# One load of all of w_in, half of batch 0 first, and a deeper ring between the two products

## The chip, the cores and the metric

The kernel runs on one core of a Trainium2 chip. TensorE (PE) multiplies matrices, VectorE (DVE), ScalarE (ACT) and GpSimd (POOL) do elementwise work, SyncE (SP) issues the transfers between the chip's memory and the core's (SBUF); products land in PSUM. The metric is the device time of one execution in microseconds (us). Before the change the median of three runs is 1023.45 us (1021.89 to 1024.68).

## The reference

The inputs are queries, keys and values of 8 batches, 8 heads, 512 local and 32 global tokens of 64 elements, and the weights of an MLP, w_in (512 x 2048) and w_out (2048 x 512), as float64. Local tokens attend to the 32 global ones and to the local ones at a distance of at most 32; global tokens attend to all.

```python
s_ll = np.where(abs(pos[:, None] - pos[None, :]) <= 32, scale * q_l @ k_l.T, -1e9)
a_l = sm(concat([scale * q_l @ k_g.T, s_ll]))        # sm: softmax with 1e-9 in the divisor
out_l = a_l @ concat([v_g, v_l])
out_g = sm(scale * q_g @ concat([k_g, k_l]).T) @ concat([v_g, v_l])
x = concat([out_g, out_l])                           # (8 * 544) tokens x 512
h = x @ w_in
y = (h * np.cos(h)) @ w_out
```

## The kernel before

Heads go in pairs, so a batch has 4 pairs, whose two heads fill 128 partitions. Tokens of a batch go in 4 query tiles of 128; a tile's keys are a window of 192 or 224 columns, so a query tile has two blocks of keys to transpose. Batches 0 and 1 (FB) have attention in float32: f_qk (L605ff) makes the scores, f_tt adds the mask and takes the negative minimum on DVE (L629), f_ex exponentiates and sums on ACT (L438), f_nm multiplies by the reciprocal of the sum on POOL (L655), f_tr transposes on PE (L670) and copies the result out of PSUM (L678), f_av multiplies with v (L698), and f_av_b splits the result into two float16 tiles, xh and xl, with the scale xsf (L715, L716). The functions fg_* do the same for global tokens. Batches 2 to 7 use float16 pairs of high and low words (sc_*, av_a) and transposing transfers.

The MLP runs over 17 chunks, 16 of 256 local tokens and one of all 256 global tokens, each in 8 steps. A step's first product, m1, is 24 matmuls (L1094: xh by wi_h, xl by wi_h, xh by wi_l) into the tile ph; then ACT (u, L1116), DVE (u, L1117), ACT (Sin, L438), POOL (square, L1129), DVE (gf, L1131), ACT (gh, L1135) and POOL (gl, L1136) make h * cos(h) in two words; the second product, m2, is 12 matmuls (L1150 to L1152). It stands `lag` = 3 steps behind m1, through a ring of 4 tiles gh and gl.

The weights are decoded from raw float64. For each piece DVE takes the maximum of its high words (raw_max, L288), then low words (L263, L266), ACT or DVE combine them (L237, L268), ACT casts the high float16 word (L281) and POOL subtracts for the low one (L231). w_in has 8 pieces of 128 x 1024, w_out 16 of 128 x 512. Raw pieces lie in places that are free until later: in the tiles of w_out (wo_h, wo_l) and in a ring of two. The pieces 6 and 7 of w_in are loaded when earlier ones have been decoded. w_in_done (L358ff) reduces the maxima of all pieces across the partitions (a matmul with ones, pm_wi) and makes from them the scale of x (xs, and f_xs's xsf, L603) by a chain of small DVE operations. Before it, no xh exists and no m1 can run.

The order of the work is written as events: `at(slot, phase, f, ...)` puts a function into a slot, one slot to a step of m1, negative ones ahead of the first. The functions are emitted by slot and phase, and a scheduler then orders each engine's instructions with this as their priority.

## Time and profile before

| | |
|---|---|
| median of three runs | 1023.45 us |
| profiled execution | 1027.77 us, span 1026.0 us |
| busy, share of the span | PE 90%, DVE 63%, ACT 63%, POOL 60% |
| granted TensorE clock, mean | 0.949 of 2.4 GHz |
| first matmul of m1 | 94.07 us |

Times in the rows below are those of the profiled execution, from its span's start. A row of the time line or of a table by lines gives busy time; idle time before an instruction stands in brackets or behind the bar, with what ended it. PE's busy time includes time at a low clock: at half the clock the same matmuls are busy twice as long, so work is compared by counts of matmuls and not by busy time alone.

### The profile page before, as it was taken

What the parts mean: (1) busy time and instruction counts of PE and PEld (TensorE: products, weight loads), DVE (VectorE), ACT (ScalarE), POOL (GpSimd) and SP (SyncE); (2) the same over time, 40 slices, a digit from 0 to 9 for tenths busy, and PEclk for the clock granted to TensorE, in tenths of its full rate; (3) what the DMA queues carried; (4) which work ended last, traced back from release to release, by engine and by line L of the source; (5) the groups of instructions that cost most, each with busy time, mean ns of one, the idle gap of its engine ahead of it and who ended that gap; (6) DMA issues with size and microseconds to landing.
All of it is one profiled execution on the core that took longest, in us unless ns stands there. A gap on an engine that the chain in (4) does not pass through costs nothing.

```text
span 1026.0 us, 20740 instructions
## 1 busy us (share of the span) xinstructions
PE 928.3 (90%) x7847; PEld 631.5 (62%) x7847; DVE 645.5 (63%) x1575; ACT 644.9 (63%) x1298; POOL 617.8 (60%) x817
## 2 busy tenths in 40 slices
PE   7864788899898889998999999998999999999996
PEld 5543456566566566766676666665666666666663
DVE  5975867467757767857585767666867644422231
ACT  6543787556667676865777577766685866444341
POOL 4472564645675956674767577767676778344442
PEclk9656898999999999999999999999999999999999
DMA  9348013044546464455545553555454423000000
GB/s 374 123 169 329 18 42 108 1 122 115 115 91 148 74 169 91 106 105 141 124 91 124 142 123 91 124 142 124 90 110 102 101 45 75 2 22 21 1 22 20
DMA packets 141147, 106.11 MB, mean 103 GB/s; under 512 B 120440, under 2 KB 120440, under 8 KB 139000
## 3 DMA queue, kind: packets, MB, share of 16 engines
q1 hardware_dynamic: 141048, 104.80, 39.8%
q8 instruction: 61, 1.00, 0.4%
q14 instruction: 38, 0.31, 0.1%
HBM read 51.82 MB, written 8.91 MB: 59 GB/s over the span
## 4 chain that ended last, share of the span: by engine, by line
PE 32%; DVE 18%; POOL 16%; DMA 13%; ACT 12%; issue 7%; SPq 1%; POOLq 0%; ACTq 0%; DVEq 0%
PE ph L1094 13%; POOL planes L881 6%; POOL t L871 6%; PE po L1152 5%; PE po L1150 5%; PE po L1151 5%; DMA qkr<-qk 5%; ACT t L438 4%; DMA vr<-v 4%; DVE kl L535 3%; POOL w L1129 2%; ACT L438 2%; DMA wo_h<-wo 2%; DVE u L1117 2%; DVE qm L494 2%
## 5 line engine op out<-in xcount | busy, mean ns | idle before, releaser
L1094 PE MATMUL ph<-xh,wi_h 128*128 128x256 f16 x1024 | 282.1, 276 | 15.9 <-DVE gf L1131 10.3
L1094 PE MATMUL ph<-xl,wi_h 128*128 128x256 f16 x1024 | 281.8, 275 | 0.9 <-DVE xl L716 0.9
L1094 PE MATMUL ph<-xh,wi_l 128*128 128x256 f16 x1024 | 281.8, 275 | 0.0
L1136 POOL TENSOR_TENSOR gl<-gf,gh 128x512 f16<-128x512 f32 x136 | 160.2, 1181 | 145.2 <-ACT gh L1135 142.5
L1094 PEld LDWEIGHTS <-wi_h 128*128 128x128 f16 x2176 | 211.5, 99 | 57.0 <-issue 23.0
L1150 PE MATMUL po<-wo_h,gh 128*128 128x512 f16 x544 | 208.6, 383 | 12.2 <-ACT o L1160 9.8
L1151 PE MATMUL po<-wo_l,gh 128*128 128x512 f16 x544 | 208.5, 383 | 0.0
L1152 PE MATMUL po<-wo_h,gl 128*128 128x512 f16 x544 | 203.1, 382 | 1.1 <-POOL gl L1136 1.0
L1129 POOL TENSOR_TENSOR w<-w 128x512 f32<-128x512 f32 x136 | 144.6, 1064 | 87.8 <-ACT w L438 84.9
L1117 DVE SCALAR_TENSOR_TENSOR u<-u,cm,ph 128x512 f32<-128x512 f32 x136 | 101.2, 744 | 132.9 <-ACT u L1116 132.7
L1131 DVE SCALAR_TENSOR_TENSOR gf<-w,ph 128x512 f32<-128x512 f32 x136 | 93.1, 685 | 108.6 <-POOL w L1129 108.0
L1135 ACT CAST gh<-gf 128x512 f16<-128x512 f32 x136 | 82.5, 613 | 120.6 <-DVE gf L1131 119.1
L438 ACT ACTIVATE t<-t,mn 128x224 f32<-128x224 f32 (+1 forms) x256 | 117.2, 459 | 50.8 <-DVE mn L809 39.8
L438 ACT ACTIVATE w<-u,ca 128x512 f32<-128x512 f32 x136 | 97.9, 721 | 81.1 <-DVE u L1117 77.0
L871 POOL TENSOR_TENSOR t<-t,sm 128x192 f32<-128x192 f32 (+1 forms) x192 | 101.0, 559 | 73.3 <-DVE sm L856 73.3
L881 POOL TENSOR_TENSOR planes<-t,planes 128x192 f16<-128x192 f32 (+1 forms) x192 | 118.3, 646 | 0.0
L1094 PEld LDWEIGHTS <-wi_l 128*128 128x128 f16 x1088 | 107.4, 99 | 16.7 <-issue 2.0
L1116 ACT ACTIVATE u<-ph,cm 128x512 f32<-128x512 f32 x136 | 92.5, 680 | 20.5 <-PE ph L1094 19.6
L1152 PEld LDWEIGHTS <-gl 128*128 128x128 f16 x544 | 53.6, 98 | 65.5 <-POOL gl L1136 2.5
L1151 PEld LDWEIGHTS <-gh 128*128 128x128 f16 x544 | 53.7, 99 | 64.0 <-issue 15.3
L1150 PEld LDWEIGHTS <-gh 128*128 128x128 f16 x544 | 53.7, 99 | 48.4 <-issue 2.7
L809 DVE CUSTOM_DVE_ANT_0 t<-ps,msk,al 128x192 f32<-128x192 f32 (+1 forms) x192 | 75.6, 427 | 5.9 <-PE ps L793 5.8
(203 smaller groups left out, 1433.6 us busy)
## 6 DMA issues: line engine op xcount, KB each, us to landing
qkr<-qk SPq DMA_DIRECT2D x24, 608.0 KB, 4.8
vr<-v SPq DMA_DIRECT2D x8, 1280.0 KB, 7.3
out<-o SPq DMA_DIRECT2D x34, 256.0 KB, 2.2
kh<-qa SPq DMA_DIRECT2D x48, 152.0 KB, 2.7
...
```

The source lines that it names most:

```text
L438: ins = nc.scalar.activation(*a, **k).ins
L871: nc.gpsimd.tensor_tensor(t[:, h], t[:, h], rb[:, h], op=ALU.mult)
L881: nc.gpsimd.tensor_tensor(lo[:, h], t[:, h], hi[:, h], op=ALU.subtract)
L1094: nc.tensor.matmul(ph[:, a], w[:, kc, f], x[:, kc, q], start=first and ip == 0, stop=last and ip == 2, skip_group_check=True,)
L1116: nc.scalar.activation(u, ph, AF.Identity, bias=m)
L1117: nc.vector.scalar_tensor_tensor(u, u, m, ph, op0=ALU.subtract, op1=ALU.subtract)
L1129: nc.gpsimd.tensor_tensor(w, w, w, op=ALU.mult)
L1131: nc.vector.scalar_tensor_tensor(gf, w, 0.5, st.pop(("ph", c, j)).rearrange("p a b -> p (a b)"), op0=ALU.subtract, op1=ALU.mult,)
L1136: nc.gpsimd.tensor_tensor(gl, gf, gh, op=ALU.subtract)
L1150: nc.tensor.matmul(po[k], gh[:, q], wo_h[:, f], start=(f == 0), stop=False)
L1151: nc.tensor.matmul(po[k], gh[:, q], wo_l[:, f], start=False, stop=False)
L1152: nc.tensor.matmul(po[k], gl[:, q], wo_h[:, f], start=False, stop=(f == NJ - 1))
```

## The change

- All 8 pieces of w_in are loaded at the start, without a wait between them: pieces 1 and 3 lie in the static tiles of the planes and of v, piece 7 in xh and xl of the second set, the others in wo_h, wo_l and one raw tile. Ahead of and between them only half the columns (352 of 608) of batch 0's queries and keys are loaded (load_half), and the mask as 16-bit words, without a copy by ACT. The second halves follow w_in.
- Batch 0's first two query tiles of all four pairs are done ahead of w_in_done; the other two, and the global tokens, stand between the first steps of m1. f_x now makes xh and xl for half a batch.
- A fence on DVE: what is emitted behind w_in_done and f_xs, up to slot 10, is ordered behind them on that engine. Only the even pieces of w_in are decoded ahead of it, the odd ones in slots 0 to 3.
- f_nm no longer multiplies the 4 tiles of scores (192 or 224 columns); it multiplies the identity by the reciprocals into 4 diagonal tiles of 128 x 128, and f_tr's transposes become float32 matmuls with these. All windows are 224 wide.
- m2 stands 11 steps behind m1 in chunks 0 and 1 and 6 afterwards; the ring of gh and gl has 11 tiles; 5 slots without m1 lie between chunks 1 and 2. w_out's maxima, scale and decode move to slots 4 to 17, batch 1 to slots 10 and on.
- Code that was switched off is gone, and a scratch area of transfers is smaller, which frees SBUF.

```diff
-WOORD = (12, 13, 14, 15, 8, 9, 10, 11, 4, 5, 6, 7, 0, 1, 2, 3)
+FTE = ((1, 1, 0, 0), (0, 0, 0, 0))
+ZH = 352
+WOORD = (8, 10, 12, 14, 9, 11, 13, 15, 0, 2, 4, 6, 1, 3, 5, 7)
+SH = 5
+LAGR = 11
+LAG = 6
+NG = 11
 MASK = -(2.0**120)
...
+            if k == 7:
+                for i, tag in enumerate(("xh", "xl")):
+                    t = ap_.tile([P, NPAIR, SL], F16, tag=tag, name=f"raw_wi7{tag}")
+                    raw = wfs["raw", k, i] = t.rearrange("p a b -> p (a b)").bitcast(I64)
+                    nc.sync.dma_start(raw, wi[kc * P : (kc + 1) * P, 1024 + 512 * i : 1536 + 512 * i])
+                return
+            if k == 1:
+                raw = plx.rearrange("p a b c d -> p (a b c d)").bitcast(I64)
+            elif k == 3:
+                raw = vhlf[:, :4096].bitcast(I64)
+            elif k == 5:
+                raw = w1.tile([P, 1024], I64, tag="raw1", name="raw_wi5", bufs=1)
+            else:
+                t, half = {0: (wo_h, 0), 2: (wo_h, 1), 4: (wo_l, 0), 6: (wo_l, 1)}[k]
                 raw = t[:, 8 * half : 8 * half + 8].rearrange("p a b -> p (a b)").bitcast(I64)
-            loads[k] = nc.sync.dma_start(raw, wi[kc * P : (kc + 1) * P, c])
+            nc.sync.dma_start(raw, wi[kc * P : (kc + 1) * P, c])
             wfs["raw", k] = raw
-
-        maxes, loads = {}, {}
 
         def w_in_max(k):
             kc = k // 2
-            if k % 2 == 0:
-                wfs["s", kc] = w1.tile([P, 3], F32, tag="ws3", name=f"ws3_{kc}", bufs=4)
...
+            sm = st.pop(("fsm", b, p, hf))
             nc.vector.tensor_scalar(sm, sm, 1e-9, None, op0=ALU.add)
             nc.vector.reciprocal(sm, sm)
-            for i in range(2):
-                for h in range(2):
-                    c = 2 * i + h
-                    nc.gpsimd.tensor_scalar(
-                        ts[i][:, h], ts[i][:, h], sm[:, c : c + 1], 1.0, op0=ALU.mult, op1=ALU.mult
-                    )
+            dg = ap_.tile(
+                [P, 4, P], F32, tag=("gt", "ptg")[(p + hf) % 2], name=f"dg_{b}_{p}_{hf}", bufs=1
+            )
+            for c in range(4):
+                nc.gpsimd.tensor_scalar(
+                    dg[:, c], ident, sm[:, c : c + 1], 1.0, op0=ALU.mult, op1=ALU.mult
+                )
+            st["dg", b, p, hf] = dg
...
-                    w = WINF[2 * hf + i][1] - P if k else P
                     for h in range(2):
-                        nc.tensor.transpose(
-                            tr[:w, 2 * i + h], ts[i][:, h, k * P : k * P + w], ident
+                        nc.tensor.matmul(
+                            tr[:w, 2 * i + h], ts[i][:, h, k * P : k * P + w], dg[:, 2 * i + h],
+                            start=(i + h == 0), stop=(i + h == 2), skip_group_check=True,
                         )
-                if k and hf == 0:
...
         def m1_d(c, j):
             w = st.pop(("u", c, j))[1]
             n = w.shape[-1]
-            gh = mp.tile([P, n], F16, tag="gh", name=f"gh_{c}_{j}", bufs=4)
-            gl = mp.tile([P, n], F16, tag="gl", name=f"gl_{c}_{j}", bufs=4)
+            s = (NS * c + j) % NG
+            pool = mp if s < 4 else mp2
+            gh = pool.tile([P, n], F16, tag="gh", name=f"gh_{c}_{j}", bufs=4 if s < 4 else NG - 4)
...
+        def fence():
+            fences.append(last("DVE"))
...
+        H = -40
+        for f, *a in (
+            (load_qk, 0, 0), (load_mask,), (load_qk, 0, 1), (w_in_load, 0), (load_qk, 0, 2),
+            (w_in_load, 1), (load_qk, 0, 3), (w_in_load, 2), (w_in_load, 3), (load_v, 0), (w_in_load, 4), (w_in_load, 5),
+            (w_in_load, 6), (w_in_load, 7),
+        ):
+            at(H, PA, f, *a)
+        for p in range(NPAIR):
+            at(H, PB, load_half, 0, p, ZH, NZ)
+        for p in range(NPAIR):
+            f_qt(H + 1 + p, 0, p, 0)
+            at(H + 2 + p, PA2, f_tr, 0, p, 0)
+            at(H + 3 + p, PA2, f_av, 0, p, 0)
+        for k in range(8):
+            at(H + 10, PA, w_in_max, k)
+            if k % 2:
+                at(H + 10, PA, w_in_piece, k - 1)
+            if k == 3:
+                at(H + 10, PA, v_a, 0)
+                at(H + 10, PA, v_b, 0)
+                at(H + 10, PA, v_c, 0)
+        at(H + 11, PA, w_in_done)
+        at(H + 11, PD, f_xs, 0)
+        at(H + 11, PE_, fence)
+        for p in range(NPAIR):
+            at(H + 12, PF, f_x, 0, p, 0)
+        for n, k in enumerate((1, 3, 5, 7)):
+            at(n, PG, w_in_piece, k)
+        at(3, PJ, zero_planes)
+        for p in range(NPAIR):
+            u = (1, 2, 4, 5)[p]
+            e = 3 + 3 * (p // 2)
+            f_qt(u, 0, p, 1, e - u)
+            at(e + 1, PA2, f_tr, 0, p, 1)
+            at(e + 1, PC, f_av, 0, p, 1)
+            at(e + 1, PF, f_x, 0, p, 1)
+        for g in range(2):
...
                 at(s, mb, m1_b, c, j)
-                at(s + 1, mc, m1_c, c, j)
-                at(s + 1, md, m1_d, c, j)
-                at(s + lag, m2, m2_a, c, j)
+                s1 = s + 1 if c > 1 else NS * c + j // 2 * 2 + 2 if c else (3, 3, 3, 6, 6, 6, 8, 8)[j]
+                at(s1, mc, m1_c, c, j)
+                at(s1, md, m1_d, c, j)
+                at(m + j, m2, m2_a, c, j)
+            at(m + NS - 1, ob, chunk_out_scale, c)
             for k in range(CT // P):
-                at(NS * c + NS - 1 + lag, ob, m2_b, c, k)
...
             if s == CE:
                 end = len(nc.cur_bb.bb.instructions)
             for _, _, f, a in sorted(ev[s], key=lambda e: e[:2]):
+                n = len(nc.cur_bb.bb.instructions)
                 f(*a)
+                if fences and s < 10:
+                    for ins in list(nc.cur_bb.bb.instructions)[n:]:
+                        if ins.engine == mybir.EngineType.DVE:
+                            tc.add_manual_dep(ins, fences[-1].name, order, reason="fence")
```

SP's queue of transfers at the start of the program, of the kernel before (wi is w_in, qkf the queries and keys of batches 0 and 1, raw_wi a raw piece; wo_h and wo_l take raw pieces of w_in here):

```order
L328 DMA wo_h<-wi 128x1024 x2
L461 DMA vr_125<-v 128x2560
L448 DMA qf_2_127<-qkf 128x608
L449 DMA kf_2_128<-qkf 128x608
L328 DMA wo_l<-wi 128x1024
L448 DMA qf_3_133<-qkf 128x608
L328 DMA wo_l<-wi 128x1024
L449 DMA kf_3_134<-qkf 128x608
L328 DMA raw_wi_137<-wi 128x1024
L328 DMA raw_wi_139<-wi 128x1024
L328 DMA wo_h<-wi 128x1024
L328 DMA wo_l<-wi 128x1024
```

and of the kernel after:

```order
L346 DMA wo_h<-wi 128x1024
L490 DMA qf_2_123<-qkf 128x352
L490 DMA kf_2_124<-qkf 128x352
L346 DMA plx<-wi 128x1024
L490 DMA qf_3_128<-qkf 128x352
L490 DMA kf_3_129<-qkf 128x352
L346 DMA wo_h<-wi 128x1024
L346 DMA vhl<-wi 128x1024
L494 DMA vr_134<-v 128x2560
L346 DMA wo_l<-wi 128x1024
L346 DMA raw_wi_137<-wi 128x1024
L346 DMA wo_l<-wi 128x1024
```

In the first excerpt whole queries and keys (608 columns) stand between the pieces, and the last two stand behind two others whose place or decode they need; in the second all pieces stand in a row with half queries and keys (352), and v ahead of the last ones.

TensorE around the scale of x and the first matmul of m1 (pm_wi: the maximum across partitions; ph_0: the first step), of the kernel before:

```order
L760 MATMUL fgtr_1_0_632<-ident,planes_g 128x128 x4
L760 MATMUL fgtr_1_1_638<-ident,planes_g 128x128
L775 MATMUL gacc_1_641<-fptg_1_631,vr_125 64x32 x8
L194 LDWEIGHTS ones
L194 MATMUL pm_wi<-d_wi,ones 128x128
L194 LDWEIGHTS ones
L194 MATMUL pm_wj<-d_wj,ones 128x128
L775 MATMUL gacc_1_641<-fptg_1_631,vr_125 64x32 x12
L1094 LDWEIGHTS wi_h
L1094 MATMUL ph_0_900<-xh_836,wi_h 128x256
```

and of the kernel after:

```order
L728 MATMUL acc_0_1_305<-ptb,vr_134 64x128 x4
L728 MATMUL acc_0_1_305<-ptb,vr_134 64x64 x2
L728 MATMUL acc_0_1_305<-ptb,vr_134 64x128 x2
L394 LDWEIGHTS ones
L394 MATMUL pm_wi<-d_wi,ones 128x256
L647 MATMUL fps_0_1_0_535<-qkr_0_114 128x224
L647 MATMUL fps_0_1_1_536<-qkr_0_114 128x224
L647 MATMUL fps_0_1_0_535<-qkr_0_114 128x224
L647 MATMUL fps_0_1_1_536<-qkr_0_114 128x224
L647 MATMUL fps_1_1_0_588<-kf_1_119,qf_1_118 128x224 x2
L1067 LDWEIGHTS wi_h
L1067 MATMUL ph_0_466<-xh_450,wi_h 128x256
```

Before, all of batch 0 and its global tokens (fgps, fgtr, gacc) stand ahead of pm_wi; after, pm_wi follows the first half's products with v (acc_0_1), and the second half's scores (fps_0_1) are mixed with the first matmuls of ph_0.

VectorE around the scale xsf (wos: a maximum of w_out; lo_wi: low words of a piece of w_in; L716 and later L746: xl), of the kernel before:

```order
L288 TENSOR_REDUCE wos<-wo_h 128x1
L1075 TENSOR_SCALAR ca_892<-hsc,pvs 128x1
L389 TENSOR_SCALAR xs<-xs,gam 128x4
L390 TENSOR_SCALAR xs_95<-xs_95,gam 128x4
L208 TENSOR_SCALAR cm_893<-ca_892 128x1
L603 TENSOR_SCALAR xsf<-xs,pvr_735 128x4
L1077 TENSOR_SCALAR cm_893<-cm_893 128x1
L1078 TENSOR_SCALAR ca_892<-ca_892 128x1
L716 SCALAR_TENSOR_TENSOR xl_837<-acc_0_314,xsf,xh_836 128x512
L716 SCALAR_TENSOR_TENSOR xl_837<-acc_1_405,xsf,xh_836 128x512
L288 TENSOR_REDUCE wos<-wo_h 128x1
L716 SCALAR_TENSOR_TENSOR xl_837<-acc_2_521,xsf,xh_836 128x512
```

and of the kernel after:

```order
L418 TENSOR_SCALAR xs<-xs,gam 128x4
L632 TENSOR_SCALAR xsf<-xs,pvr_447 128x4
L1042 TENSOR_SCALAR ca_460<-hsc,pvs 128x1
L267 TENSOR_SCALAR lo_wi_496<-plx 128x1024
L270 TENSOR_SCALAR lo_wi_496<-plx 128x1024
L661 ISA t_0_2_542,mn_0_1_541<-fps_0_1_0_535,msk,alf 128x224
L661 ISA mn_0_1_541 128x1
L661 ISA t_0_2_542,mn_0_1_541<-fps_0_1_1_536,msk,alf 128x224
```

Before, the chain is mixed with maxima of w_out and the xl of all four pairs follow; after, the chain stands alone, and the decode of an odd piece and the mask of the second half's scores come behind it, ahead of the first xl.

## Rows read from the trace of the kernel before

**Rows 1.** The page's first parts: busy time of each engine over the span, and the GB/s that the DMA engines moved in 40 slices of 25.65 us.

```profile
PE 928.3 (90%) x7847; PEld 631.5 (62%) x7847; DVE 645.5 (63%) x1575; ACT 644.9 (63%) x1298; POOL 617.8 (60%) x817
...
GB/s 374 123 169 329 18 42 108 1 122 115 115 91 148 74 169 91 106 105 141 124 91 124 142 123 91 124 142 124 90 110 102 101 45 75 2 22 21 1 22 20
```

**Rows 2.** The table by stretches of the whole trace. Columns: stretch in us, its length, busy us and number of instructions of PE, PE's weight loads, DVE, ACT and POOL, the granted TensorE clock, DMA share, GB/s.

```profile
0.00:40.00 40.00, 29.82 (x144) 21.39 (x144) 28.39 (x105) 21.90 (x65) 17.97 (x43) 0.93 0.73 290
40.00:100.00 60.00, 36.01 (x262) 23.75 (x263) 45.39 (x118) 28.48 (x53) 29.84 (x40) 0.53 0.63 230
100.00:120.00 20.00, 12.41 (x82) 9.21 (x79) 16.35 (x59) 13.55 (x32) 7.94 (x12) 0.83 0.09 28
120.00:240.00 120.00, 108.42 (x839) 74.39 (x839) 80.42 (x191) 82.55 (x158) 64.41 (x85) 0.93 0.24 77
240.00:400.00 160.00, 143.87 (x1291) 97.90 (x1289) 112.40 (x271) 109.07 (x229) 107.67 (x145) 0.98 0.52 114
400.00:960.00 560.00, 541.80 (x4874) 369.26 (x4872) 347.17 (x814) 368.45 (x733) 368.01 (x475) 0.99 0.41 92
960.00:1016.00 56.00, 55.96 (x367) 35.62 (x364) 14.63 (x21) 20.85 (x31) 21.98 (x20) 1.00 0.03 10
1016.00:1026.00 10.00, 0.00 (x0) 0.00 (x0) 0.75 (x1) 0.00 (x0) 0.00 (x0) 0.76 0.17 52
```

**Rows 3.** The same table for the instructions of line L1094 alone (the first product): busy us of its matmuls (x records) and of its weight loads, the granted clock, DMA share, GB/s.

```profile
0.00:120.00 120.00, 10.48 (x72) 7.90 (x72) 0.72 0.57 216
120.00:240.00 120.00, 40.25 (x315) 31.55 (x316) 0.93 0.24 77
```

**Rows 4.** The same for line L1150, a third of the second product.

```profile
120.00:240.00 120.00, 20.23 (x52) 5.18 (x52) 0.93 0.24 77
```

**Rows 5.** The chain that ended last, near its end: start us, us, what. The first product's 24 matmuls of two neighbouring steps.

```profile
997.77 2.62 PE ph L1094 x24
...
1002.98 2.62 PE ph L1094 x24
```

**Rows 6.** The time line of PE: start us, us from the first start to the last end, engine, line, operation, out<-in, shapes, number of records, and in brackets the idle time before with its releaser.

```profile
94.07 0.37 PE L1094 MATMUL ph<-xh,wi_h 128*128 128x256 f16 x1 [5.57 <-ACT xh L715]
...
106.37 2.88 PE L614 MATMUL fps<-qkr 64*128 64x192 f32 x16
...
129.00 2.06 PE L698 MATMUL acc<-fpt,vr 128*64 128x128 f32 x32
...
138.13 0.60 PE L670 MATMUL ftr<-ident,t 128*128 128x128 f32 x4
```

**Rows 7.** The time line of SP's queue and of DVE: the issues of the last two pieces of w_in and the maximum of the last.

```profile
23.54 0.33 SPq L328 DMA_DIRECT2D wo_h<-wi  x1
39.78 0.33 SPq L328 DMA_DIRECT2D wo_l<-wi  x1
...
47.35 1.21 DVE L288 TENSOR_REDUCE ws<-wo_l 128x1 f32<-128x1024 f32 x1
```

**Rows 8.** The time line around the scale of x (DVE, and the ACT instruction that it releases).

```profile
87.00 0.29 DVE L196 TENSOR_REDUCE r_wi<-pm_wi 128x1 f32<-128x128 f32 x1 [2.46 <-PE pm_wi L194]
...
87.40 0.14 DVE L311 TENSOR_SCALAR wr_i<-r_wi 128x1 f32<-128x1 f32 x1
87.58 0.15 DVE L312 TENSOR_SCALAR wr_i<-wr_i 128x1 uint32<-128x1 uint32 x1
...
93.07 0.22 DVE L603 TENSOR_SCALAR xsf<-xs,pvr 128x4 f32<-128x4 f32 x1
...
93.33 1.84 ACT L715 ACTIVATE xh<-acc,xsf 128x512 f16<-128x512 f32 x3 [7.29 <-DVE xsf L603]
```

**Rows 9.** The page's costliest groups, the instructions of one MLP step on DVE and ACT: line, engine, operation, out<-in, shapes, count | busy us, mean ns of one | idle us before, releaser.

```profile
L1117 DVE SCALAR_TENSOR_TENSOR u<-u,cm,ph 128x512 f32<-128x512 f32 x136 | 101.2, 744 | 132.9 <-ACT u L1116 132.7
L1131 DVE SCALAR_TENSOR_TENSOR gf<-w,ph 128x512 f32<-128x512 f32 x136 | 93.1, 685 | 108.6 <-POOL w L1129 108.0
L1135 ACT CAST gh<-gf 128x512 f16<-128x512 f32 x136 | 82.5, 613 | 120.6 <-DVE gf L1131 119.1
...
L438 ACT ACTIVATE w<-u,ca 128x512 f32<-128x512 f32 x136 | 97.9, 721 | 81.1 <-DVE u L1117 77.0
...
L1116 ACT ACTIVATE u<-ph,cm 128x512 f32<-128x512 f32 x136 | 92.5, 680 | 20.5 <-PE ph L1094 19.6
```

**Rows 10.** The time line of DVE and POOL at two decodes of w_in.

```profile
35.36 0.90 DVE L263 TENSOR_SCALAR lo_wi<-raw_wi 128x1024 uint16<-128x1024 uint16 x1
...
59.20 3.33 DVE L263 TENSOR_SCALAR lo_wi<-raw_wi 128x1024 uint16<-128x1024 uint16 x1
...
59.38 2.56 POOL L231 TENSOR_TENSOR wi_l<-y_wi,wi_h 128x256 f16<-128x256 f32 x4
```

**Rows 11.** The table by stretches for 40 to 100 us in three slices, columns as in rows 2.

```profile
40.00:60.00 20.00, 16.37 (x95) 9.85 (x96) 16.51 (x46) 12.93 (x28) 13.03 (x19) 0.50 0.50 169
60.00:80.00 20.00, 10.24 (x97) 7.18 (x95) 17.64 (x34) 8.92 (x10) 13.55 (x17) 0.59 0.42 141
80.00:100.00 20.00, 9.40 (x72) 6.72 (x73) 11.23 (x40) 6.63 (x16) 3.25 (x5) 0.51 0.96 380
```

**Rows 12.** Groups of instructions by line and shape on DVE in the first 240 us, columns as in rows 9.

```profile
L629 DVE CUSTOM_DVE_ANT_0 t<-fps,msk,alf 128x224 f32<-128x224 f32 x48 | 19.9, 446 | 0.2
...
L288 DVE TENSOR_REDUCE wos<-wo_h 128x1 f32<-128x512 f32 x8 | 5.5, 682 | 6.3 <-DMA wo_h<-wo 6.1
```

More of the change, by code (lines that the diff above doesn't have):

```diff
@@ L607, in f_qk @@
             pt = [
[L608 removed]
+                ps.tile(
+                    [P, 2, FW], F32, tag="ph" if (b, hf, h) == (0, 0, 1) else "att",
+                    name=f"fps_{b}_{p}_{hf}_{h}",
+                )
+                for h in range(2)
             ]
@@ new lines, in f_g, with load_mask, zero_planes, slot0 @@
+        def f_g(u, b, g):
+            at(u, PG, fg_a, b, g)
+            at(u, PG, fg_b, b, g)
+            at(u + 1, PG, fg_c, b, g)
+            at(u + 1, PG, fg_d, b, g)
+        def load_mask():
+            nc.sync.dma_start(msk.bitcast(U16), mask)
+        def fence():
+            fences.append(last("DVE"))
+        def zero_planes():
+            for i in range(4):
+                nc.gpsimd.memset(planes[i], 0.0)
+        def slot0(c):
+            return NS * c + (SH if c > 1 else 0)
@@ new lines, in body, with last @@
+        fences = []
+        def last(e):
+            return [i for i in nc.cur_bb.bb.instructions if i.engine == getattr(mybir.EngineType, e)][-1]
+        H = -40
[7 more added lines that the diff above has]
+            at(H, PB, load_half, 0, p, ZH, NZ)
```

450 lines of the change are left out of this document (180 added, 270 removed).

## The prediction

> **What bounds the kernel now.** I read the table by stretches first [rows 2]. From 960 us on TensorE is never idle, and 400 to 960 us has it busy 97%; the last 10 us have no matmul at all. So the end of the run is set by how much TensorE work is left at 400 us, and time can be won only where TensorE waits or runs slowly, which is before 400 us. The granted clock tells the second half of the story: 0.93 in the first 40 us, 0.53 from 40 to 100 us, 0.98 and more after 240 us. A clock of 0.53 is nearer to the level of 1.2 GHz than to 2.4 GHz. Over the span the engines are busy 90% (PE) and 60 to 63% (the three others) [rows 1].
>
> Next I counted work instead of busy time. One step of the MLP is 24 matmuls of the first product (2.62 us at full clock) and 12 of the second, a period of 5.21 us, so the second half takes 2.59 us [rows 5]. Until 240 us the trace has 72 + 315 = 387 matmuls of L1094 [rows 3], 390 with those that the trace misses, or 16.25 steps, and 52 of L1150 [rows 4], 4 in a step, which with a few lost records makes 13.5 steps. At full clock that is 16.25 x 2.62 + 13.5 x 2.59 = 77.5 us. The attention of batches 0 and 1 by unit rows [rows 6]: a score matmul is two records of 2.88/16 = 0.18 us, a transpose one of 0.15, an attention-times-v product two of 2.06/32 = 0.064. The code issues 64, 128 and 128 of them for two batches: 23 + 19 + 16 = 58 us, and about 14 for the global tokens, 72 together or 36 per batch. With 2 us of batch 2 the work done by 240 us is worth 151.5 us. TensorE thus lost 88 us before 240 us, where the change acts.
>
> The reason stands in two views. w_in's last two pieces are issued at 23.54 and 39.78 us, the last maximum runs at 47.35 [rows 7], the cross-partition maximum is read at 87.00, the scale of x is there at 93.07 [rows 8], and the first MLP matmul starts at 94.07 [rows 6]. Until then the MLP has no work, and the second product waits longer, since its weights are decoded after.
>
> **The change part by part.**
>
> *Loads (stage A).* SP now issues 1.44 MB of half queries and keys, 0.23 MB of mask, 8.39 MB of w_in and 1.31 MB of v with no wait between: 11.4 MB. At the 374 GB/s of the first slice [rows 1] that is 30.4 us; with 3 to 4 us to start and land, 34 us. By the 290 GB/s of the first 40 us [rows 2] it is 39 us plus the same: these are my bounds, 34 and 43, and I take 34 because the queue is no longer interrupted. VectorE has to do by then 8 maxima at 1.21 [rows 7], four even pieces at 3 us, 16 score reductions at 0.446 [rows 12] and small ones, about 31 us in all, so it may be late by a few. Behind the last maximum stands a chain of some 18 dependent small operations at the 0.18 us of [rows 8] (87.40, 87.58), a hop through PE, and the rest of one decode: 7 us. The scale is ready at about 41 us, against 93.07. The fence only keeps other DVE work behind this chain; what it holds back (second half scores, odd pieces) has no one waiting before 41 us. The mask copy dropped from ACT is counted at nothing, since ACT's work there lies beside the loads.
>
> *From 41 us to the first m2 (stage B).* In PE's order twelve steps of m1, the second half of batch 0 and its global tokens come before the first second product. TensorE's work in it is 12 x 2.62 + 18 + 4 = 53 us. VectorE's is larger: 12 steps of 0.744 + 0.685 us = 17.1 [rows 9]; four odd pieces with three 1024-wide operations between 0.90 [rows 10] and 1.21 us [rows 7], 12; 16 maxima of w_out at 0.68, 10.9; 16 score reductions at 0.446, 7.1 [rows 12]; some 24 small ones (copies, xl, sums, scales), 10: 57 us. ScalarE's is about the same: 12 steps of 0.680 + 0.721 + 0.613 = 24.2 [rows 9], and 30 for exponentials, table loads and casts. VectorE was busy 76% in 40 to 100 us and 67% in 120 to 240 [rows 2], with the same kind of work in both; I take 75%, so 76 us, and the first m2 starts near 117 us instead of 127. From 0.82 (100 to 120 us) to 0.67 the range is 70 to 85 us. The 8.39 MB of w_out queue behind w_in and the second halves (1.05 MB): by the same 374 GB/s they are in by about 63 us, before their scale is wanted at step 9, so I cost them at nothing; if they were late, the first m2 would be, not m1.
>
> *To the state that the kernel before has at 240 us (stage C).* What is left is 4.25 steps of m1 (11), 13.5 of m2 (35), batch 1 (36) and batch 2's 2 us: 84 us. The normalising matmul adds to it. It is a full float32 product where a transpose was: a score product of 192 columns takes 2 x 0.18 us, so 128 columns about 0.24, against 0.15 [rows 6]: +0.09 on 64 in each batch, 6 us here. The bounds are nothing (if a plain matmul costs what a transpose does) and +0.21 each, 13 us (if it costs a whole score product). The Trainium skill (TensorE: Matmul & The Clock Gate, section "Terms") calls the transpose mode four times faster for float32. By it a product would take 0.60 us and stage C 29 us more, but the score rows give a ratio of 1.6, so I don't follow it. POOL scales 128 columns instead of 192 or 224, which is cheaper by a little. So 90 us of work. In 120 to 240 us the kernel before did 315/24 = 13.1 steps of m1, 13 of m2 and about 32 us of attention, 100 us of work in 120, a share of 0.84 [rows 2 to 4]. 90/0.84 = 107 us: the state is reached at 224 us, 16 to 17 us sooner. With 0.80 and 0.90 it is 112 and 100 us.
>
> *After it.* The deeper ring of g and the lag of 6 or 11 steps let m2 wait less, while attention beyond it stands in PE's order as before; 240 to 400 us lost about 15 us, 400 to 960 about 23 us [rows 2]. What of the first bit is regained I count at nothing, since ACT and POOL each have as much work per step there as PE; if the ring does cover it, it is worth up to 10. The last 66 us keep.
>
> Sum: profiled run 1027.8 - 17 = 1011 us. It lies 4.3 us above the median of the runs shown, so 1006 us.
>
> **The rivals.**
>
> *The ring and the early start pay in full.* Stage B at 0.82 ends at 111 us; with m2 eleven steps behind, PE always finds ready work and stage C runs at 0.97 as 400 to 960 us did [rows 2]: 93 us, state at 204, 36 us sooner, and the ring wins back two thirds of the 15 us lost in 240 to 400. 1023.5 - 46 = 977. For it: the weights' decodes no longer stand between m1 and m2. Against: VectorE and ScalarE are still the fuller ones.
>
> *The gain is given back.* Batch 2's attention has the same chain of ACT, POOL and transposing DMAs; if it sets the time after 240 us, PE arrives early and waits there. The end stays, near 1023. For it: the lost 15 us in 240 to 400 with the other engines at 67 to 70% [rows 2].
>
> *Slower: TensorE stays at the low clock in stage B.* From 40 to 100 us the granted clock was 0.50, 0.59 and 0.51, with PE busy only half to four fifths of these slices [rows 11]. Stage B now has PE waiting on VectorE for small pieces again. If all its 53 us of work run at 1.2 GHz they take 106, the stage ends at 147 and the state is reached 14 us later than before: 1023.5 + 14 = 1037. It decides from a share x of low clock where 53(1 + x) is over 76, x = 0.43, and all gain is gone at 53(1 + x) = 93, x = 0.75. For it: that stretch of before. Against: 100 to 120 us had 0.83 as soon as m1 ran.
>
> *Slower: decode meets POOL.* The low-word step at 35.36 us took 0.90 us, the same at 59.20 took 3.33 us, beside 2.56 us of POOL's subtractions [rows 10]. The Trainium skill (GPSIMD Engine Reference, section "Specifications") says that GpSimd's SBUF interfaces are shared with VectorE; the trace agrees in this row, 3.33 against 0.90 us. If all 8 pieces of w_in and, at half the size, 16 of w_out paid the 2.43 us, it would be 39 us of VectorE; two thirds of that, 26, outweigh the gain of 17: 1023.5 + 9 = 1032.
>
> **How the numbers follow.** Main case 0.45, its own range from 70 + 100 us (state at 211, 994 us) to 85 + 112 (238, 1021); a w_in that lands at 43 us puts 9 us on either. Full pay 0.20 (977). Given back 0.08 (1023). Low clock 0.17 (1037). Port 0.10 (1032). The range of 8 in 10 reaches from 974, which leaves part of the full pay outside, to 1034, which leaves most of the low clock's worst. A change under 0.3% (1020.4 to 1026.5) can't be told from none. Faster: 0.43 of the main case, 0.20, 0.02 of given back, 0.03 and 0.02 where the slow rivals take only part: 0.70. Same: 0.02 + 0.05 + 0.01 + 0.01 = 0.09. Slower: 0.01 + 0.13 + 0.07 = 0.21.
>
> **What would show it.** Right: xsf and the first L1094 at 38 to 46 us, the first L1150 at 110 to 125, 13 steps of m2 done by 225 us, a normalising matmul near 0.24 us, the table by stretches from 400 us on as before. Wrong: a w_in that lands after 45 us; a granted clock under 0.7 between 45 and 110; low-word steps of 3 us; TensorE idle between 240 and 400 us behind batch 2's scores, by more than the 15 us of before.

## The result, and the profile after

The changed kernel takes 1035.9 us (median of 9 runs, 1032.36 to 1037.81), the kernel before 1027.73 us on the same chip (9 runs, 1021.89 to 1032.29): ratio 1.008, 95% interval [1.0058, 1.0102]. It is slower by some 8 us, where 1006 us and a gain of 17 were forecast. The span of the profiled execution is 1033.2 us, against 1026.0.

The page's first part and its GB/s row, to be read against [rows 1], and the table by stretches, against [rows 2, 11]:

```profile
PE 929.4 (90%) x7974; PEld 636.2 (62%) x7974; DVE 652.4 (63%) x1573; ACT 644.3 (62%) x1302; POOL 609.9 (59%) x812
...
GB/s 359 184 241 66 101 49 108 41 70 120 137 107 122 103 133 123 87 131 133 124 90 123 141 122 91 123 141 113 101 103 111 79 63 75 2 22 1 21 22 20
```

```profile
0.00:40.00 40.00, 24.43 (x161) 19.67 (x162) 29.69 (x90) 23.71 (x57) 14.23 (x33) 0.87 0.91 351
40.00:100.00 60.00, 40.96 (x316) 33.02 (x316) 51.63 (x124) 38.38 (x74) 37.95 (x55) 0.83 0.40 132
100.00:120.00 20.00, 16.96 (x162) 11.28 (x162) 8.38 (x22) 9.02 (x16) 6.31 (x7) 0.74 0.29 94
120.00:240.00 120.00, 109.59 (x814) 69.99 (x813) 82.47 (x218) 69.43 (x152) 57.45 (x84) 0.99 0.22 74
240.00:400.00 160.00, 131.89 (x1216) 90.42 (x1215) 119.60 (x286) 111.95 (x235) 101.01 (x139) 0.95 0.55 122
400.00:960.00 560.00, 541.52 (x4921) 372.52 (x4916) 344.90 (x815) 370.94 (x742) 370.78 (x479) 0.99 0.42 94
...
40.00:60.00 20.00, 12.55 (x81) 9.85 (x81) 19.69 (x62) 8.64 (x11) 10.64 (x16) 0.74 0.30 106
60.00:80.00 20.00, 9.55 (x61) 7.01 (x60) 19.24 (x32) 14.91 (x31) 12.40 (x14) 0.74 0.71 236
80.00:100.00 20.00, 18.86 (x177) 16.16 (x178) 12.70 (x33) 14.84 (x33) 14.91 (x26) 1.00 0.18 54
```

From 400 to 960 us nothing changed: TensorE is busy 541.5 us here and 541.8 before. In the early stretches TensorE has a higher granted clock (0.83 against 0.53 in 40 to 100 us). The stretch that lost is 240 to 400 us: TensorE is busy 131.9 us where it was 143.9.

Counting steps of the two products says the same more exactly. The first two rows are L1067, the first product (24 matmuls a step), against [rows 3]; the last is L1125, a third of the second product (4 a step), against [rows 4]:

```profile
0.00:120.00 120.00, 33.89 (x238) 25.43 (x239) 0.83 0.55 199
120.00:240.00 120.00, 22.00 (x176) 16.42 (x173) 0.99 0.22 74
```

```profile
120.00:240.00 120.00, 21.90 (x64) 5.59 (x64) 0.99 0.22 74
```

By 240 us 414/24 = 17.25 steps of the first product are done (16.25 before) and 64/4 = 16 of the second (13.5). That is 2.6 + 6.5 us of TensorE work, less 2 of batch 2 that before has done by then: a lead of about 7 us. Batch 1's global tokens, whose last products (gacc, below) run at 240.6 to 242.5 us, take about 2 more off it, so it is 5 to 7 us. The same two lines to 400 us, first of the changed kernel, then of before (L1094 and L1150):

```profile
0.00:400.00 400.00, 120.52 (x912) 92.46 (x912) 0.92 0.45 130
...
120.00:400.00 280.00, 46.94 (x128) 12.05 (x128) 0.96 0.41 101
```

```profile
0.00:400.00 400.00, 116.89 (x924) 92.04 (x925) 0.88 0.45 133
...
120.00:400.00 280.00, 54.09 (x140) 13.88 (x140) 0.96 0.40 98
```

Now 912/24 = 38.0 and 128/4 = 32 steps stand against 38.5 and 35: 1.3 + 7.8 = 9 us behind. So some 14 to 16 us are lost between 240 and 400 us. TensorE is idle for 28 us there instead of 16, which makes 12 of them; its granted clock is 0.95 instead of 0.98, which over 132 busy us is another 4 by estimate.

What is handed over at 240 us shows in the table for 200 to 240 us, of the kernel before and then of the changed one:

```profile
200.00:240.00 40.00, 37.23 (x293) 25.48 (x292) 26.26 (x49) 23.98 (x41) 17.46 (x17) 1.00 0.44 134
```

```profile
200.00:240.00 40.00, 40.00 (x275) 23.63 (x275) 18.98 (x50) 9.78 (x24) 5.52 (x13) 1.00 0.26 76
```

TensorE is busy for all of the 40 us, and ScalarE and GpSimd nearly stand still. In the time line of GpSimd and of PE of the changed kernel the place can be seen; then the last low plane of batch 1's x on DVE, of the changed kernel and of before:

```profile
214.57 1.41 POOL L688 TENSOR_SCALAR dg<-ident,fsm 128x128 f32<-128x128 f32 x4 [2.71 <-PE ftr L703]
225.09 0.72 POOL L780 TENSOR_SCALAR planes_g<-planes_g,gsm 128x544 f32<-128x544 f32 x1 [9.11 <-DVE gsm L779]
...
232.47 0.22 PE L507 MATMUL pm_qk<-d_qk,ones 128*128 128x128 bf16 x1
232.53 1.98 PE L703 MATMUL ftr<-dg,t 128*128 128x128 f32 x16
...
240.63 0.66 PE L803 MATMUL gacc<-fptg,vr 128*64 128x32 f32 x16
241.65 0.89 PE L803 MATMUL gacc<-fptg,vr 128*64 128x32 f32 x24
242.48 0.26 PE L820 MATMUL ps<-kh,qa 128*128 128x192 f16 x1
```

```profile
243.36 0.48 DVE L746 SCALAR_TENSOR_TENSOR xl<-acc,xsf,xh 128x256 f16<-128x256 f32 x1 [0.16 <-ACT xh L745]
```

```profile
196.03 0.75 DVE L716 SCALAR_TENSOR_TENSOR xl<-acc,xsf,xh 128x512 f16<-128x512 f32 x1
```

The normalising diagonals of batch 1's last pair (dg) are ready at 216 us, but their product (ftr) stands in TensorE's order behind second products and behind a small matmul of batch 2, and runs at 232.53. Batch 1's x is complete at 243.4 us instead of 196, and batch 2's first score runs at 242.5 instead of 222.1. TensorE did second products first, and ScalarE and GpSimd had little to do.

Then the waits of TensorE from 240 to 400 us, of the changed kernel and of before (who waited for whom; us in total, times, longest):

```profile
PE ph L1067 <- DVE gf L1106: 13.4, 5, 4.6
PE acc L909 <- DMA ptb<-plx: 6.6, 5, 2.3
PE ps L821 <- DMA kl<-kl: 2.7, 2, 1.4
```

```profile
PE ph L1094 <- DVE gf L1131: 6.2, 3, 2.8
PE ps L792 <- DVE qm L494: 3.4, 1, 3.4
```

The lead is returned mainly in front of gf, near the end of a step's elementwise work, and of batch 2's planes (ptb).

### The profile page after: what moved, and what is told of

Its sections match the earlier page's. It is cut to its first block, busy times and chain, and to the rows that moved or that the text cites. A ratio compares the mean times of both kernels' runs of the same rounds, so it can differ in the third digit from the quotient of the medians.

```text
span 1033.2 us, 21011 instructions
## 1 busy us (share of the span) xinstructions
PE 929.4 (90%) x7974; PEld 636.2 (62%) x7974; DVE 652.4 (63%) x1573; ACT 644.3 (62%) x1302; POOL 609.9 (59%) x812
## 4 chain that ended last, share of the span: by engine, by line
PE 37%; DVE 17%; POOL 16%; DMA 11%; ACT 11%; issue 6%; SPq 1%; POOLq 0%; ACTq 0%; DVEq 0%
PE ph L1067 15%; PE po L1126 5%; PE po L1127 5%; PE po L1125 5%; POOL t L867 5%; POOL plx L872 5%; DMA qkr<-qk 4%; ACT t L464 3%; DVE kl L566 3%; DMA vr<-v 3%; POOL w L1104 2%; ACT L464 2%; PE ftr L703 2%; DVE u L1090 2%; POOL gl L1111 1%
## 5 line engine op out<-in xcount | busy, mean ns | idle before, releaser
L1067 PE MATMUL ph<-xh,wi_h 128*128 128x256 f16 x1024 | 284.1, 279 | 35.7 <-DVE gf L1106 29.4
L1067 PE MATMUL ph<-xl,wi_h 128*128 128x256 f16 x1024 | 285.4, 279 | 1.5 <-DVE xl L746 1.4
L1067 PE MATMUL ph<-xh,wi_l 128*128 128x256 f16 x1024 | 285.3, 279 | 0.0
L1067 PEld LDWEIGHTS <-wi_h 128*128 128x128 f16 x2176 | 214.1, 100 | 87.6 <-issue 32.2
L1111 POOL TENSOR_TENSOR gl<-gf,gh 128x512 f16<-128x512 f32 x136 | 160.4, 1180 | 124.6 <-ACT gh L1110 123.6
L1125 PE MATMUL po<-wo_h,gh 128*128 128x512 f16 x544 | 204.6, 381 | 10.6 <-DVE o L1133 6.2
L1127 PE MATMUL po<-wo_h,gl 128*128 128x512 f16 x544 | 206.8, 381 | 2.0 <-POOL gl L1111 2.0
L1104 POOL TENSOR_TENSOR w<-w 128x512 f32<-128x512 f32 x136 | 144.2, 1061 | 99.6 <-ACT w L464 99.4
L867 POOL TENSOR_TENSOR t<-t,sm 128x192 f32<-128x192 f32 (+1 forms) x192 | 104.3, 576 | 66.2 <-DVE sm L857 66.2
L1067 PEld LDWEIGHTS <-wi_l 128*128 128x128 f16 x1088 | 108.7, 100 | 17.5 <-issue 2.1
L872 POOL TENSOR_TENSOR plx<-t,plx 128x192 f16<-128x192 f32 (+1 forms) x192 | 115.7, 634 | 2.3 <-ACT plx L870 2.3
L1125 PEld LDWEIGHTS <-gh 128*128 128x128 f16 x544 | 52.7, 98 | 55.7 <-issue 8.6
L837 DVE CUSTOM_DVE_ANT_0 t<-ps,msk,al 128x192 f32<-128x192 f32 (+1 forms) x192 | 76.0, 427 | 11.0 <-PE ps L821 10.7
```

What stands on the lines that cost most here:

```text
L867: nc.gpsimd.tensor_tensor(t[:, h], t[:, h], rb[:, h], op=ALU.mult)
L872: nc.gpsimd.tensor_tensor(lo[:, h], t[:, h], hi[:, h], op=ALU.subtract)
L1067: nc.tensor.matmul(ph[:, a], w[:, kc, f], x[:, kc, q], start=first and ip == 0, stop=last and ip == 2, skip_group_check=True,)
L1104: nc.gpsimd.tensor_tensor(w, w, w, op=ALU.mult)
L1111: nc.gpsimd.tensor_tensor(gl, gf, gh, op=ALU.subtract)
L1125: nc.tensor.matmul(po[k], gh[:, q], wo_h[:, f], start=(f == 0), stop=False)
```

## The experiments

All ratios are to the kernel before, with their 95% interval. Unless said otherwise an edit is made to the changed kernel; it stands beside 1.008. SH is the number of slots by which chunk 2 and batch 2, with all that follow, stand later; LAG is how many slots the second product follows behind the first from chunk 2 on. The theories of the first rounds: SUPPLY, later TAIL (batch 1's attention got too late, and the MLP runs out of x), LAG (the second product too far behind), MATMUL (the normalising product costs by itself); then GAP (batch 2's attention needs more slots without a first product beside it) and LEAD (the distance between batch 2's attention and chunk 2's products). An expectation gives the ratio that each theory would make.

**The parts of the change alone.** no_fence lets VectorE take any work before the scale of x:

```diff
-                if fences and s < 10:
+                if fences and s < -100:
```

> Edit: the fence on VectorE is left out. If the fence holds back work that the second half of batch 0 wants, xsf comes later than 45.6 us but the first second product sooner than 128 us: ratio 1.002 to 1.006. SUPPLY: the first 130 us hardly matter, since x of batch 1 is what is waited for at 243 us: 1.006 to 1.010.

Measured: 1.0222 [1.0189, 1.0255]. The first second product runs at 137.84 us instead of 127.99, and from there on the program lists TensorE's work in the same order. Both theories had expected 1.002 to 1.010. A delay of 10 us there arrives at the end as 14. So the fence pays, and time lost in this stretch does reach the end.

plain_transposes takes the normalisation out of the transposing matmul again:

```diff
-                nc.gpsimd.tensor_scalar(dg[:, c], ident, sm[:, c : c + 1], ...)
+                nc.gpsimd.tensor_scalar(ts[i][:, h], ts[i][:, h], sm[:, c : c + 1], ...)
...
-                nc.tensor.matmul(tr[:w, 2 * i + h], ts[i][:, h, ...], dg[:, 2 * i + h], ...)
+                nc.tensor.transpose(tr[:w, 2 * i + h], ts[i][:, h, ...], ident)
```

> Edit: the normalisation goes back to GpSimd's multiplication of the scores and the transposes to TensorE's transpose mode; order and windows stay. MATMUL: 128 products cost 0.25 instead of about 0.15 us, 12 us over both batches, and all of it comes back: ratio 0.997 to 1.000. SUPPLY: in batch 1's chain each of 8 groups of 8 products gets 0.8 us shorter and GpSimd's four multiplications 0.3 us longer, 4 us in all: 1.003 to 1.007. LAG: 1.008.

Measured: 1.0027 [0.9999, 1.0054], 5 us better, between what MATMUL and SUPPLY gave, although the first second product came 11 us later (139.15 us). b1_earlier_lag_3_transposes puts the same edit on b1_earlier_lag_3 (below):

> Edit: the one before, with the plain transposes as well. MATMUL as a loss of its own: another 0.005, ratio 0.985 to 0.990. If plain_transposes gained only because the order behind it came out otherwise: within 0.002 of the one before, or worse, as the first second product came at 139 us with it instead of 128.

Measured: 1.0064 [1.0032, 1.0096] against 0.9953 [0.9933, 0.9974] without the edit: there the transposes lose 11 us. An edit with both signs has no fixed price of its own, so MATMUL falls. In both runs other instructions of TensorE change places too; that the order makes the sign is likely, but not shown.

**Batch 1 sooner, or chunk 2 and batch 2 later.** b1_two_slots_earlier loads and starts batch 1 two slots sooner:

```diff
-            f_g(7 + g, 0, g)
+            f_g(6 + g, 0, g)
...
-            at(8 + p // 2, PJ, load_qk, 1, p)
-            u = 10 + 2 * p
+            at(7 + p // 2, PJ, load_qk, 1, p)
+            u = 8 + 2 * p
```

> Edit: batch 0's global tokens one slot earlier, batch 1's loads one and its attention two slots earlier; nothing else. In the changed kernel's trace the last xl of batch 1 comes at 243 us (before: 196), ScalarE and GpSimd are nearly idle from 206 to 244 us, and TensorE then waits 28 us between 240 and 400 us (before: 16). Theory SUPPLY (batch 1's attention stands behind 15 steps of m1, so the MLP runs out of x): last xl of batch 1 10 us or more earlier, ratio to the kernel before 1.000 to 1.004 instead of 1.008. Theory LAG (the larger distance of m2, 6 steps, is what costs) and theory MATMUL (the normalising matmul's extra TensorE work is what costs): ratio stays at 1.008, within 0.002.

Measured: 1.002 [1.0003, 1.0038]. Batch 1's x is there at 225.5 us, 18 sooner, and 6 us are won, as SUPPLY had it. last_pair_one_slot moves batch 1's last pair alone one slot sooner, its products with v (f_av) and its xh and xl (f_x) likewise:

```diff
-                at(u + 3, PA2, f_tr, 1, p, hf)
+                at(u + 3 - p // 3, PA2 if p < 3 else PE_, f_tr, 1, p, hf)
...
```

> Edit: of the changed kernel only the last pair of batch 1 is touched: its normalising matmuls, its products with v and its xh and xl stand one slot earlier. In the changed kernel's order these matmuls stand directly behind pm_qk of batch 2's second pair, which runs at 232.47 us, though their diagonal tiles are there at 216 us; with the edit they stand ahead of it. TAIL: last xl of batch 1 by 235 us instead of 243, ratio 0.995 to 1.002. If the longer gap helped in another way (batch 2's attention spread over more slots): 1.005 to 1.010.

Measured: 1.0061 [1.0033, 1.009]. The x came 9.4 us sooner (233.95 us), but 2 us were won at most, which the intervals don't tell from none; TAIL's 0.995 to 1.002 is missed. So a late x isn't all of the loss: gap_8_lag_6, next, has x at 232.2 us and a ratio of 0.9936.

m2_three_behind has SH 8 and LAG 3 for 5 and 6, gap_8_lag_6 SH 8 alone:

> Edit: from chunk 2 on m2 stands 3 steps behind m1 instead of 6, and the gap without m1 behind chunk 1 is 8 slots instead of 5, so that m2's slots stay where they were. LAG: 3 steps of m2 (7.8 us), by which the changed kernel is behind at 960 us, come back: ratio 1.000 to 1.002. SUPPLY: chunk 2 gets no x sooner and its slots come later: ratio 1.006 to 1.015. MATMUL: 1.008.

> Edit: the gap without m1 is 8 slots as in m2_three_behind, but m2 stays 6 steps behind. Theory LAG (m2 held back while TensorE waits for the other engines between 240 and 400 us): the gain of m2_three_behind is gone, ratio 1.006 to 1.013, and m2 is again 5 to 6 steps behind m1 at 400 us. Theory GAP (batch 2's attention got three slots more without m1 beside it): the gain stays, ratio 0.997 to 1.002.

Measured: 0.9987 [0.9965, 1.0009] and 0.9936 [0.9913, 0.996]. With 8 slots a lag of 6 is better than 3, so LAG falls; the three slots alone are worth 1.4%, more than GAP had given them. The two edits on top of the earlier batch 1 are b1_earlier_lag_3 (SH 8, LAG 3) and b1_earlier_gap_8 (SH 8):

> Edit: b1_two_slots_earlier and m2_three_behind together. If SUPPLY and LAG are two losses: 1.008 - 0.006 - 0.0095, ratio 0.990 to 0.995. If they are one loss seen from two sides: 0.997 to 1.001, not better than m2_three_behind alone.

> Edit: b1_two_slots_earlier and gap_8_lag_6 together. If an earlier end of batch 1 and the longer gap cure different losses: 1.008 - 0.006 - 0.0144, ratio 0.986 to 0.990. If the longer gap cures the same wait: 0.992 to 0.996.

Measured: 0.9953 [0.9933, 0.9974], and 0.9925 [0.9888, 0.9963]. The gains don't add up: the earlier batch 1 and the three slots cure in the main the same loss. m2_from_step_9, also on the earlier batch 1, starts the second product early too (LAGR 9, SH 6, LAG 3, maxima and decodes of w_out one or two slots sooner):

> Edit: b1_two_slots_earlier, m2 9 instead of 11 steps behind in chunks 0 and 1 and 3 later, gap 6 slots, w_out's maxima one slot and its scale and decode two slots earlier. If the backlog of m2 that runs alone from 206 to 244 us is what starves ScalarE and GpSimd (SUPPLY), it is two steps shorter and chunk 2 starts about 5 us sooner than in b1_earlier_lag_3: ratio lower by 0.002 to 0.006. If the decode of w_out is what limits VectorE before the first second product: no gain or up to 0.005 worse.

Measured: 0.9982 [0.9961, 1.0004]. The first second product runs at 104.64 us, 23 sooner than in the changed kernel, and the time is no better than with b1_earlier_lag_3, which has SH 8: the earlier second product won nothing here.

**Which part of the three slots.** mlp_later_only moves the MLP alone from chunk 2 on by three slots, mlp_later_b2_as_was (shown) the MLP and the batches behind batch 2:

```diff
-SH = 5
+SH = 8
...
-            t = 16 * (b - 1) + T0[b > 2] + SH
+            t = 16 * (b - 1) + T0[b > 2] + (5 if b == 2 else 8)
```

> Edit: the gap is 8 slots for the MLP alone; attention of all batches from 2 on stays in its slots, so that it leads the MLP by 3 slots more until the end. LEAD: 0.988 to 0.996, and TensorE's waits for transposes of planes and for ph between 240 and 400 us fall from 20 us to under 12. TAIL: 1.004 to 1.012.

> Edit: the gap without m1 is 8 slots for the MLP and for batches 3 to 7, but batch 2's attention stays where the changed kernel has it. gap_8_lag_6 gave 0.9936. Theory TAIL (batch 2's early work slows batch 1's last pairs; moving it away let x of batch 1 come at 232 instead of 243 us): the gain goes, last xl of batch 1 at 240 us or later, ratio 1.004 to 1.010. Theory LEAD (in the changed kernel chunk 2 and 3's m1 run beside batch 2's attention, which lacks a lead, so TensorE waits in order behind late scores and transposes): the gain stays or grows, ratio 0.989 to 0.996, last xl as it may.

Measured: 1.0198 [1.0154, 1.0242] and 1.0073 [1.0047, 1.01], against 0.9936 where batch 2 moves along. Distance to the MLP alone, LEAD, loses. In mlp_later_b2_as_was the last x of batch 1 comes at 242.5 us and the ratio is in TAIL's range; mlp_later_only, with x at 244.0 us, is worse than either theory gave. The reverse, attention later with the MLP as it is, wasn't run, and neither was an earlier batch 2 in the changed kernel itself. gap_11_lag_6 has three slots more, SH 11:

> Edit: a gap of 11 slots without m1, m2 6 steps behind from chunk 2 on. LEAD: with m2 of chunk 1 ending at slot 26 and chunk 2 beginning at slot 27, TensorE has less to do beside the attention, 3 slots of 2.6 us each are lost again: ratio 0.996 to 1.004. TAIL: no further gain and no loss, 0.992 to 0.997.

Measured: 1.0227 [1.0194, 1.026], which neither theory had; TensorE waits 10.7 us for batch 2's d_qk between 240 and 300 us.

**The other way.** What was still open: is it idle ScalarE and GpSimd before 240 us (IDLE), or a batch 2 too close upon batch 1 (ROOM)? On the earlier batch 1, SH is 4 or 3, or batch 2 alone is moved from 5 to 3:

> Batch 1's attention stands as in b1_two_slots_earlier (ratio 1.002), and everything from chunk 2 and batch 2 on is one slot earlier (SH 4 for 5). In TensorE's order batch 2's first scores then stand behind 12 steps of the second product instead of 16, so they start some 8 us sooner (233 us for 242). IDLE (what costs is that ScalarE and GpSimd stand idle at 206 to 240 us, because TensorE works off second products then; any earlier work for them is gained): they get work sooner, ratio 0.990 to 0.999, ScalarE busy for 260 us or more by 400 us. ROOM (what costs is that batch 2 and chunk 2 follow too close upon batch 1's tail, on the three other engines; 7 and 8 slots gave 0.992): one slot less is worse, 1.004 to 1.010, ScalarE under 256 us by 400 us.

> The same with two slots less (SH 3). IDLE: 0.988 to 0.999, as for 4, unless TensorE's order holds the first scores back again (they stand behind 16 steps of the second product, as with 5). ROOM: worse than with 4, 1.008 to 1.025.

> Batch 2's attention alone two slots earlier (3 for 5), the MLP and the later batches as in b1_two_slots_earlier. Its last scores then stand at step 25 of the first product instead of 28. IDLE: its x is ready earlier, chunk 3 is not late, 0.992 to 1.000. ROOM: batch 2 lies on batch 1's tail: 1.006 to 1.020, and TensorE waits for DVE's gf at 240 to 320 us by more than the 13 us of after.

Measured: 0.9976 [0.9955, 0.9998]; 1.0 [0.9983, 1.0018]; 0.9999 [0.9972, 1.0026]. ROOM expected a loss in all three and falls. IDLE's ranges hold 0.9976 and 0.9999, and the 1.0 of b1_earlier_gap_3 lies just outside. The table by stretches of b1_earlier_gap_4 and then of gap_8_lag_6 shows two different gains:

```profile
200.00:240.00 40.00, 39.64 (x333) 26.04 (x333) 26.71 (x61) 18.19 (x40) 7.15 (x14) 1.00 0.36 109
240.00:400.00 160.00, 140.99 (x1246) 94.68 (x1244) 119.36 (x285) 111.30 (x232) 108.83 (x151) 0.94 0.53 120
```

```profile
200.00:240.00 40.00, 40.00 (x324) 25.54 (x324) 15.58 (x40) 10.60 (x25) 4.45 (x12) 1.00 0.15 51
240.00:400.00 160.00, 141.82 (x1306) 97.44 (x1304) 119.29 (x317) 121.51 (x254) 115.42 (x156) 0.96 0.59 137
```

With 4 slots ScalarE does 18.2 us of work in 200 to 240 us (13.1 in b1_two_slots_earlier, 9.8 in the changed kernel) and then no more than there, 111 in the next 160. With 8 slots it does 10.6, and then 121.5. So IDLE is at most a part: the step from b1_two_slots_earlier to b1_earlier_gap_4 is worth 4.5 us (1.002 to 0.9976), and gap_8_lag_6 has the same idle stretch as the changed kernel and none of its loss.

The last two, b1_earlier_gap_8_pairs and b1_earlier_gap_7, are the earlier batch 1 with 8 slots and its last two pairs a slot sooner, and with 7.

> Edit: b1_earlier_gap_8, with the last two pairs' normalising matmuls, products with v and xh, xl one slot earlier as well. TAIL: x of batch 1 already comes at 226 us there, a few more us: ratio 0.988 to 0.993. If the rest is set by batch 2's attention: 0.992 to 0.997, no better than b1_earlier_gap_8 (0.9925).

> Edit: b1_earlier_gap_8 with a gap of 7 slots. With batch 1 two slots earlier its tail needs the longer gap less, and a gap of 11 was worse than 8 by 0.029: ratio 0.988 to 0.993 if 8 is already too long, 0.993 to 1.000 if the gap still shields the tail.

Measured: 0.9912 [0.9879, 0.9945] and 0.9922 [0.9893, 0.9951]. Both beat the kernel before by 8 to 9 us, and the changed one by 16 to 17. Their intervals hold the 0.9925 of b1_earlier_gap_8, so they don't tell the theories apart.

One setting, then, gives these ratios, with the same instructions in another order:

| SH | changed kernel | with batch 1 two slots sooner |
|---|---|---|
| 3 | not run | 1.000 |
| 4 | not run | 0.9976 |
| 5 | 1.008 | 1.002 |
| 7 | not run | 0.9922 |
| 8 | 0.9936 | 0.9925 |
| 11 | 1.0227 | not run |

## Why the prediction was wrong

**Stage A** (34 us for w_in, the scale at 41) was nearly right. On SP's queue, DVE and PE, against [rows 6 to 8]:

```profile
14.42 0.35 SPq L335 DMA_DIRECT2D raw_wi7xl<-wi  x1
...
37.69 0.66 DVE L292 TENSOR_REDUCE wm<-raw_wi7xl 128x1 f32<-128x512 f32 x1
...
45.56 0.59 DVE L632 TENSOR_SCALAR xsf<-xs,pvr 128x4 f32<-128x4 f32 x1
```

```profile
46.71 0.80 PE L1067 MATMUL ph<-xh,wi_h 128*128 128x256 f16 x3 [3.94 <-ACT xh L745]
...
127.99 0.61 PE L1125 MATMUL po<-wo_h,gh 128*128 128x512 f16 x2
```

The loads ran at 351 GB/s, between the two bounds, and the last maximum ended at 38.4 us. The chain behind it took 7 us, as counted. The scale came 4.6 us late, and still 47.5 us before the old one.

**Stage B** (57 us of VectorE at 75%, 76 us, first second product at 117) was mis-sized by a little at both terms. The table for the stretch between scale and second product:

```profile
45.56:127.99 82.43, 63.61 (x559) 49.48 (x559) 61.05 (x142) 51.39 (x98) 45.82 (x60) 0.83 0.38 127
```

VectorE had 61.05 us of work and was busy 74%: 82.4 us, inside the 70 to 85 given. With the late start the second product begins at 128, 11 us behind the forecast and 1 us behind the kernel before. At 40 to 80 us VectorE is full, 19.69 and 19.24 of 20 us.

**Stage C.** The normalising product was forecast at 0.24 us; 16 records take 1.98 us, two records a product, 0.25 us. The 0.15 of a transpose was read from a group of 4, whose last record's end weighs more. Groups of 8 compare better, in the changed kernel, two records a product, and in plain_transposes, one record a transpose:

```profile
235.86 1.05 PE L703 MATMUL ftr<-dg,t 128*128 128x128 f32 x8
```

```profile
215.24 1.04 PE L702 MATMUL ftr<-ident,t 128*128 128x128 f32 x8
```

That is 0.26 to 0.13 us, a ratio of 2.0 and not 1.6, and 8 us instead of 6 for 64 of them. The Trainium skill (TensorE: Matmul & The Clock Gate, section "Terms") calls the transpose mode four times faster for float32; the two traces give 2.0, and the measurement decides. The second products came nearly as counted: 13.5 steps of the second were done at 227 us, where 224 was forecast. But a part of batch 1's attention was still behind them, until 243 us, and by all of TensorE's work the lead of 17 us was 5 to 7. The 10 to 12 that are missing are the 11 of stages A and B.

**"After it"** is the step that failed: "What of the first bit is regained I count at nothing", as if at least the 16 to 17 us would stay. It put the loss behind 240 us at nothing; the traces show one of 14 to 16 us in 240 to 400 us. Together with the 11 of stages A and B this makes the error of 25 us (17 ahead forecast, 8 behind measured).

The prediction counted TensorE's work done and called an equal count the same state. The other engines have their own. Over the first 240 us, of before, of the changed kernel and of gap_8_lag_6:

```profile
0.00:240.00 240.00, 186.67 (x1323) 128.75 (x1324) 170.55 (x471) 146.47 (x306) 120.15 (x178) 0.82 0.41 147
```

```profile
0.00:240.00 240.00, 191.94 (x1448) 133.95 (x1450) 172.17 (x451) 140.55 (x297) 115.93 (x176) 0.91 0.39 136
```

```profile
0.00:240.00 240.00, 190.74 (x1505) 134.59 (x1506) 168.50 (x446) 142.37 (x301) 118.39 (x176) 0.93 0.37 132
```

ScalarE did 140.55 us of work in the changed kernel and 146.47 before. In the whole run it has about the same to do, 644.3 and 644.9 us, so at 240 us it is 5 us behind and not ahead. GpSimd's 115.93 and 120.15 can't be read that way: its whole work shrank from 617.8 to 609.9 us, so that 494 us are left against 498. TensorE's lead was made mostly of second products, whose inputs had long been there, while batch 1's attention, and with it batch 2's, stood behind them. In TensorE's order batch 1's first scores had moved from step 3 of the first product to step 15. The prediction priced their TensorE time and not that move.

But this state isn't the loss by itself. gap_8_lag_6 has at 240 us much the same counts, and by its steps a lead too, 438/24 = 18.25 of the first product and 60/4 = 15 of the second, and at 400 us it is still ahead of before, with 981/24 = 40.9 and 136/4 = 34:

```profile
0.00:240.00 240.00, 58.40 (x438) 43.92 (x438) 0.93 0.37 132
0.00:400.00 400.00, 124.75 (x981) 97.78 (x982) 0.94 0.46 134
```

```profile
0.00:240.00 240.00, 20.09 (x60) 5.26 (x60) 0.93 0.37 132
0.00:400.00 400.00, 49.16 (x136) 12.70 (x136) 0.94 0.46 134
```

That is 2.4 x 2.62 - 2.6 = 3.6 us, where the changed kernel is 9 us behind. What the lead is worth is decided by the spacing of what comes after it.

What is shown of this: the loss of 14 to 16 us between 240 and 400 us, the idle stretch ahead of it and its place in the order, and that order alone moves the time by 3% (0.9936 to 1.0227 in one column of the table). That the idle stretch makes the loss isn't shown. In the profiles of the 18 kernels run, of before and of the changed one, the ratio follows the work that ScalarE has done by 400 us (correlation -0.93): 243 to 244 us in the two slowest (1.022 and 1.023), 252.5 in the changed kernel, 264 to 266 in the four fastest (0.991 to 0.994). mlp_later_only is the exception (252 us at 1.020). That is a tally of progress and not yet a cause. Why ScalarE does 121 us of work in 160 with 7 or 8 slots, and 112 with 5, stays open, and with it the cause of the loss: LAG, MATMUL, LEAD and ROOM were each expected to explain it and didn't, and TAIL and IDLE explain a part at most. Against the x alone speaks also b1_earlier_gap_3, with x at 237.4 us and a ratio of 1.000, beside b1_two_slots_earlier, with x at 225.5 us and 1.002.

The rivals. "The gain is given back" (0.08) came nearest, with TensorE waiting between 240 and 400 us, but stopped at no loss; 0.08 was too little for it, and none of the rivals let the start of batch 2 be later than before. "Pays in full" failed with stage B. "Low clock": 0.74 at 40 to 80 us, where 0.50 and 0.59 stood before, 1.00 at 80 to 100 and 0.83 over stage B, whose length VectorE's work explains at the forecast share. "Decode meets POOL": the low-word steps of w_out sum to 24.4 us, against 17.9 before (those of w_in 14.2 against 15.1), so it cost some 6 us of VectorE and not 26. Of the signs that I named as wrong, one came: TensorE idle from 240 to 400 us by 28 us instead of 16, though more of it in front of gf than of batch 2's scores.
